# Group 2's second product over 16 row pairs, and five smaller moves, in a fused attention and MLP block

## The chip, the cores and the metric

The kernel runs on one core of a Trainium2 chip. The metric is device time in microseconds (us): the median of several executions of the whole program, from its first to its last instruction. The engines of a core work side by side, each through its own list of instructions in a fixed order, and wait for each other by semaphores: TensorE (PE in the profile; PEld is its loading of the stationary operand), VectorE (DVE), ScalarE (ACT), GpSimd (POOL), and SyncE (SP), which issues most of the DMAs here. A DMA queue is also worked off in order of issue. SBUF is the memory on the chip, with 128 partitions; PSUM is the small memory that matmuls write.

## The reference

One transformer block over 2048 tokens of width 576. LayerNorm, attention over a dilated window of 8 earlier positions (every second one), 32 heads of 18; the projection `wo`; a residual sum; LayerNorm again; an MLP of 4608 columns with GELU (its tanh form); another residual sum.

```python
    def _A_ref(x, wqkv, wo):
        B, S, D = x.shape
        H = 32; Dh = D // H
        W, dil = 8, 2
        qkv = (lambda x, *d: x.transpose(*d))((x @ wqkv).reshape(B, S, 3, H, Dh), 2, 0, 3, 1, 4)
        q, k, v = qkv[0], qkv[1], qkv[2]
        scale = Dh ** -0.5
...
        logits = jnp.einsum("bhsd,bhswd->bhsw", q, kg) * scale
        logits = jnp.where(mask[None, None, :, :], logits, -1e9)
        attn = _softmax(logits, axis=-1)
        o = jnp.einsum("bhsw,bhswd->bhsd", attn, vg)
        return (lambda x, *d: x.transpose(*d))(o, 0, 2, 1, 3).reshape(B, S, D) @ wo

    def _B_ref(x, w1, b1, w2, b2):
        y = _layernorm(x, axis=-1)
        h = _gelu(jnp.einsum("bsd,df->bsf", y, w1) + b1)
        return jnp.einsum("bsf,fd->bsd", h, w2) + b2

    x = A_x
    h = x + _A_ref(_layernorm(x, axis=-1), A_wqkv, A_wo)
    h2 = h + _B_ref(_layernorm(h, axis=-1), B_w1, B_b1, B_w2, B_b2)
    return h2
```

## The kernel before

The 2048 tokens are 16 tiles of 128. A tile j holds every sixteenth token, so that a position two tokens earlier lies in tile j-2, and the window of a tile is made of tiles of the same parity. `kv_ring` holds K and V of the eight even and of the eight odd tiles; after a tile's turn its K or V row is read again from `kv_dram`, shifted by one token (`halo`). The tiles are worked in `ATT_ORDER` (even ones from 14 down, then odd ones from 15 down), two at a time: `GROUPS[0]` is (14, 12), then (10, 8), (6, 4), (2, 0), (15, 13), (11, 9), (7, 5), (3, 1). The first two tiles are called A[0] and A[1] below, the next A[2] and A[3].

The whole order is written by hand, engine by engine, as Python lists of calls that are interleaved with the matmuls.

First come 24 visits (`qd` 0 to 23, L994 to 1000) of two QKV products each. A product of 64 rows of contraction uses half of TensorE, and two such halves run side by side; `visit` (L242) sends the first half of each product (`phase` 0), then the second halves (`phase` 1), which use the other rows. A `marker`, an empty instruction in GpSimd's list, stands between the halves: it waits for the end of a first half, and the second half waits for it. A dictionary gives what is put in: `hooks` between the two halves, `between` behind a second half, `after` behind the visit. ScalarE copies each product from PSUM (L322). In the last visits the attention output o of A[0] and A[1] is turned round by TensorE (`tr_o`, L433), with a copy of its last 64 columns twice side by side (`o_tail`, by ScalarE); Wo follows as a third product of visits 17 and 20; then LN2, the second LayerNorm (`ln2`, `ln2_rstd`, `ln2_norm`: VectorE's statistics, GpSimd's power of -0.5, called the root here, and ScalarE's normalisation), and its output `hn` is turned (`tr_h`, L556) in visits 22 and 23. `transpose_tail` uses 12 matmuls for this: 8 for 512 columns, and 4 for the last 64 columns, which are written once to each half of the partitions.

Then the loop over the groups (L1038), with k = 0 to 7. A group's stage is W1 with GELU (`mlp1`, four visits), Wo of the next group, and W2. In the lists, c and d are the next group's tiles, e and f those of the group after. VectorE meanwhile computes the attention of e and f: `att_qk_a` (products of q and K), `att_qk_b` (sums over the head's width), `att_max` (the maximum and its subtraction), ScalarE's exponential (`exps`), `att_den` (the sum and its reciprocal), then, one group later, `pv_sum` (the products with V), which gives o. `send_o` writes o to DRAM in two stores and `read_o` reads it back turned round (`dma_tr_o` does both), into `oT`, for Wo. LN2 goes the same way: `ln2_h` (h = the projection plus x, by VectorE), `ln2_act` (its sums by ScalarE, its root by GpSimd), `ln2_send` and `ln2_in`. A dependency written by hand keeps the next `att_qk_a` behind the root of LN2 (L354).

W2 is done in two ways. Groups 0 and 1 use 36 row blocks with two matmuls each per tile (`mlp2`, L598). From group 2 on, `mlp2_fast` (L711) takes the blocks in pairs and uses seven products instead of eight, in the manner of Strassen and Winograd, for the first `rows` pairs; the other pairs, up to 18, are done plainly, with 8 matmuls a pair (`plain`). The seven products need sums of blocks of W2 (`w2_sums`, made once) and of h (`h_sums`, made in each group), by VectorE. `t_slot` and `s_slot` say where these are kept. `ROWS` gives 12 pairs for group 2, 16 for groups 3 to 5 and 18 for the last two. `steps` is the order: a tuple is a product and its range of pairs; "wo" is the Wo visit; "b", "d" and "f" are ScalarE's copies of a PSUM bank to the bank in which another product goes on (L782); "hc", "h", "6", "7", "in", "exp", "4" and "3" are places where the lists in `x` are called; "rest" and "o0" are ScalarE's copies of results, "o1" VectorE's sums `o_sb` (L724). Group 2 does product 1 first and Wo behind it; groups 3 to 6 do Wo first.

```python
        ROWS = {2: 12, 3: 16, 4: 16, 5: 16, 6: NM, 7: NM}
...
            if 3 <= k < 7:
                mlp2_fast(g, rows, (s, p, q, r), wo, x, True)
                p, q, r, s = q, r, p, s
            else:
                mlp2_fast(g, rows, (q, p, r, s), wo, x)
```

W2 is loaded in seven parts (`load_w2`). The last one, the row blocks 32 to 35, is issued in group 0, in the list `m1[1]`, between the first and the second half of PV of the group's second tile d.

## Time and profile before

| | |
|---|---|
| median of 3 executions | 360.77 us (360.17 to 361.07) |
| profiled execution, its own time | 361.01 us |
| its span | 359.2 us |
| PE busy, matmuls | 353.4 us (98%), 4953 |
| DVE busy | 295.8 us (82%) |
| ACT busy | 235.8 us (66%) |
| POOL busy | 47.3 us (13%) |
| DMA traffic | 46.29 MB, mean 129 GB/s |

The profile is of one execution. A busy TensorE isn't TensorE at its best, since matmuls overlap: the end of a matmul is modelled, and a short wait shows only as a longer distance between two starts. In a timeline, a row stands for several instructions of one kind, with the start of the first and the time to the end of the last; the number behind x is their count, and a bracket gives the idle time of the engine before it and what ended it. `L228` is the matmul in `phase`, `L605` and `L693` are those of W2, `pq`, `pm`, `pw` and `po` the PSUM tiles of QKV, W1, Wo and W2.

By the windows of the trace, W1 of groups 2, 3 and 4 takes 17.79, 17.80 and 17.78 us (142.38 to 160.17, 178.88 to 196.68 and 214.72 to 232.50), so a group takes some 36 us.

### The profile page before, as it was taken

The numbers are of one execution on the slowest core, as the hardware profiler recorded it, in microseconds if no ns is written. First come the engines' busy times: TensorE is split into PE (matmuls) and PEld (weight loads), VectorE is DVE, ScalarE is ACT, GpSimd is POOL, SyncE is SP. The second block draws the span as 40 slices with busy tenths as digits, with TensorE's granted clock in tenths as the row PEclk, the third lists the DMA queues.
The fourth block names the chain that finished last, engine by engine and source line by source line (L and its number), as shares of the span: only waits on it lengthen the run. The fifth ranks groups of instructions, "written<-read, shape, count | busy, mean of one in ns | idle before, by whom it ended". The sixth has DMA issues, their size and how long they took to land.

```text
span 359.2 us, 11579 instructions
## 1 busy us (share of the span) xinstructions
PE 353.4 (98%) x4953; PEld 289.5 (81%) x4953; DVE 295.8 (82%) x416; ACT 235.8 (66%) x524; POOL 47.3 (13%) x61
## 2 busy tenths in 40 slices
PE   8999999999999999999999999999999999999996
PEld 4777978887788877887788778877887788778874
DVE  5999999999989989998799899989998998520431
ACT  4889757897647783668566956685669566706620
POOL 2241003000212020201200211021102110210000
PEclk9999999999999999999999999999999999999999
DMA  7997799955737584722553545344555253253001
GB/s 242 328 296 168 186 248 294 387 188 137 153 71 123 164 222 84 126 71 49 118 85 82 100 110 84 77 114 108 85 90 102 57 86 56 55 120 51 4 1 34
DMA packets 63492, 46.29 MB, mean 129 GB/s; under 512 B 32192, under 2 KB 61760, under 8 KB 63440
## 3 DMA queue, kind: packets, MB, share of 16 engines
q1 hardware_dynamic: 59472, 41.50, 43.6%
q0 software_dynamic: 3744, 3.84, 9.9%
q8 instruction: 38, 0.62, 0.8%
q10 hardware_dynamic: 224, 0.22, 0.3%
q14 instruction: 14, 0.11, 0.1%
HBM read 23.38 MB, written 12.42 MB: 100 GB/s over the span
## 4 chain that ended last, share of the span: by engine, by line
PE 72%; DVE 20%; DMA 4%; SPq 1%; ACT 1%; issue 1%; DVEq 0%; ACTq 0%
PE pm L228 34%; PE po L693 25%; PE po L605 9%; PE pw L228 4%; DVE prod L361 3%; DVE ln_stats L148 3%; DVE prod L409 3%; DVE prod L352 3%; DVE prod L415 2%; DMA oT<-td 2%; DMA x_all<-in_A_x_dram 1%; ACT h_all L586 1%; SPq L104 1%; DMA td<-q_all 1%; DVE ln_mv L149 1%
## 5 line engine op out<-in xcount | busy, mean ns | idle before, releaser
L228 PE MATMUL pm<-hnT,w_sb 64*128 64x256 bf16 x2304 | 143.0, 269 | 0.0
L586 ACT ACTIVATE h_all<-pm,b_sb 128x256 f16<-128x256 f32 (+1 forms) x288 | 108.4, 495 | 51.2 <-PE pm L228 50.5
L228 PEld LDWEIGHTS <-w_sb 64*128 64x128 bf16 x2304 | 111.7, 94 | 15.1 <-issue 1.7
L693 PEld LDWEIGHTS <-h_all 128*128 128x128 f16 x480 | 46.2, 98 | 13.7 <-issue 1.6
L228 PE MATMUL pq<-wq_sb,xnT 64*128 64x288 bf16 x720 | 54.9, 283 | 0.7 <-DMA wq_sb<-in_A_wqkv_dram 0.2
L228 PEld LDWEIGHTS <-xnT 64*128 64x128 bf16 x864 | 43.4, 94 | 10.9 <-issue 1.4
L361 DVE TENSOR_TENSOR prod<-prod 128x2304 bf16<-128x2304 bf16 (+1 forms) x64 | 44.2, 691 | 2.1
L352 DVE TENSOR_TENSOR prod<-kv_ring,q_all 128x4608 bf16<-128x4608 bf16 x16 | 40.8, 2550 | 2.8 <-POOL ln_rstd L500 2.5
L409 DVE TENSOR_TENSOR prod<-kv_ring,probs 128x4608 bf16<-128x4608 bf16 x16 | 40.9, 2558 | 1.1 <-DMA kv_ring<-kv_dram 0.6
L228 PE MATMUL pm<-hnT,w1h_sb 64*128 64x256 bf16 x288 | 39.2, 269 | 0.0
L693 PE MATMUL po<-w2a_sb,h_all 128*128 128x288 bf16 (+1 forms) x262 | 35.8, 286 | 0.0
L415 DVE TENSOR_TENSOR prod<-prod 128x2304 bf16<-128x2304 bf16 (+1 forms) x32 | 33.9, 1058 | 1.1
L605 PEld LDWEIGHTS <-h_all 128*128 128x128 bf16 x288 | 27.8, 98 | 7.9 <-issue 1.0
L693 PEld LDWEIGHTS <-kv_ring 128*128 128x128 f16 x252 | 24.6, 98 | 6.3 <-DVE kv_ring L673 0.2
L605 PE MATMUL po<-w2a_sb,h_all 128*128 128x288 bf16 x224 | 28.5, 286 | 0.0
L228 PE MATMUL pq<-wqh_sb,xnT 64*128 64x288 bf16 x144 | 27.6, 283 | 0.0
L795 POOL DMA_DIRECT2D x_all<-o_sb x12 | 10.7, 888 | 126.1 <-PE pw L228 73.1
L500 POOL TENSOR_TENSOR ln_rstd<-ln_var,mhalf 128x1 f32<-128x1 f32 x13 | 10.3, 792 | 80.8 <-ACT ln_var L499 80.8
L228 PE MATMUL pw<-wo_sb,oT 64*128 64x288 bf16 x256 | 19.6, 283 | 0.7 <-DMA oT<-td 0.7
L693 PE MATMUL po<-w2b_sb,h_all 128*128 128x288 bf16 (+1 forms) x122 | 19.7, 286 | 0.1
L673 DVE TENSOR_TENSOR kv_ring<-h_all 128x1536 f16<-128x1536 f16 (+3 forms) x9 | 6.8, 760 | 15.8 <-ACT h_all L586 15.8
L161 POOL TENSOR_TENSOR ln_rstd<-ln_veps,mhalf 128x1 f32<-128x1 f32 (+2 forms) x14 | 13.2, 951 | 47.6 <-DVE ln_nmean L489 30.1
(115 smaller groups left out, 401.3 us busy)
## 6 DMA issues: line engine op xcount, KB each, us to landing
w_sb<-in_B_w_dram SPq DMA_DIRECT2D x6, 768.0 KB, 6.1
kv_ring<-kv_dram SPq DMA_DIRECT2D x28, 144.0 KB, 2.3
kv_dram<-kv_ring SPq DMA_DIRECT2D x13, 288.0 KB, 3.7
w2a_sb<-in_B_w_dram SPq DMA_DIRECT2D x3, 1008.0 KB, 10.5
x_all<-in_B_b_dram SPq DMA_DIRECT2D x15, 144.0 KB, 4.1
td<-q_all SPq DMA_DIRECT2D x14, 144.0 KB, 2.0
td<-hn SPq DMA_DIRECT2D x14, 144.0 KB, 1.8
x_all<-h POOLq DMA_DIRECT2D x14, 144.0 KB, 4.6
```

The lines of the kernel that those rows point to most:

```text
L148: nc.vector.bn_stats(out=stats[:, i, c, :], in_=src[:, c * HALF:(c + 1) * HALF])
L161: nc.gpsimd.tensor_tensor(out=rstd[:], in0=veps[:], in1=mhalf[:].to_broadcast([P, n]), op=ALU.pow)
L228: last = nc.tensor.matmul(duo["g"][r ^ swap][i], lhsT=lhsT, rhs=rhs, start=(swap == 0 and i == 0 and kt == 0), stop=(swap == 1 and kt == K ...
L352: ins = nc.vector.tensor_tensor(out=prod[:], in0=k_ring[j % 2], in1=q_all[:, j, :].unsqueeze(1) .to_broadcast([P, W, D]), op=ALU.mult).ins
L361: nc.vector.tensor_tensor(out=prod[:, :, o * H:o * H + n], in0=prod[:, :, a * H:a * H + n], in1=prod[:, :, c * H:c * H + n], op=ALU.add)
L409: nc.vector.tensor_tensor(out=prod[:].rearrange("p w (d h) -> p w d h", h=H), in0=v_ring[j % 2].rearrange("p w (d h) -> p w d h", h=H), in ...
L415: nc.vector.tensor_tensor(out=prod[:, 0:n, :], in0=prod[:, 0:n, :], in1=prod[:, n:2 * n, :], op=ALU.add)
L500: ins = nc.gpsimd.tensor_tensor(out=rstd[:], in0=var[:], in1=mhalf[:], op=ALU.pow).ins
L586: pace[0] = nc.scalar.activation(out=hT(grp)[:, f, 0:N], in_=ps[:, r, i * N:(i + 1) * N], func=ACT.Gelu_apprx_tanh, bias=b1_sb[:, f:f + 1] ...
L605: nc.tensor.matmul(banks[half], lhsT=hT(grp)[:, f, i * P:(i + 1) * P], rhs=w2_rows(f)[:, half * HALF:(half + 1) * HALF], start=(f == 0), s ...
L693: nc.tensor.matmul(bank, lhsT=l, rhs=r, start=start, stop=stop, skip_group_check=True)
L795: nc.gpsimd.dma_start(out=x_of(j), in_=o_of.pop(j), accum_op=ALU.add)
```

## The change

Six things are changed.

- Group 2 uses 16 pairs in the seven products, with Wo first, as groups 3 to 5 do; the order of `steps` and the rotation of PSUM banks are now one for groups 2 to 6. For this the W2 sums of pairs 12 to 15 are all made in group 2, the second tile's QK product goes behind LN2's h and the h sums, and the h sums of pairs 12 to 15 have a place: three slots, two of them in rows of `x_all` that are not yet loaded again (`spare`). The load of x into these rows goes behind the last product of group 2.
- The maximum of the first tile e is taken alone, ahead of the second tile's QK product, in groups 2 to 5; that of f behind it.
- The load of W2's last four row blocks, half of `w2b_sb` (`load_w2(6)`), goes behind the stores and the turned read of o of tile d in group 0.
- `tr_o` of A[0] goes from between the halves of visit 16 to behind the first second half.
- `tr_h` of A[0] goes from between the halves of visit 22 to behind the first second half, and the exponential of A[2] behind the other.
- `tr_h` uses 10 matmuls; the last 64 columns come from a copy, twice side by side, that GpSimd makes (`h_tail`), behind second halves of visits 20 and 22. `transpose_tail` is gone.

```diff
-    def transpose_tail(pair, src):
-        for kt in range(KF):
...
+    def h_tail(j):
+        o_tails[j] = qp.tile([P, 2, HP], BF16, tag="tail", name="tail", bufs=2)
+        nc.gpsimd.tensor_copy(out=o_tails[j][:], in_=hn[j][:, KF * P:D].unsqueeze(1).to_broadcast([P, 2, HP]))
...
     def tr_h(j, tag):
         pair = psum_pair(tag, "h_pt")
-        transpose_tail(pair, hn.pop(j)[:])
+        transpose_in(pair, hn.pop(j)[:], o_tails.pop(j)[:].rearrange("p r c -> p (r c)"))
         nc.scalar.copy(**turned(hnT_slot(j), pair))
...
         if not ring1_free[0]:
-            return q_all[:, 15 - 2 * i, (m0 - SR) * P:(m1 - SR) * P].bitcast(F16).rearrange("p (m c) -> p m c", c=P)
+            rows, j = ((q_all, 15), (x_all, 10), (x_all, 8))[i] if spare[0] else (q_all, 15 - 2 * i)
+            return rows[:, j, (m0 - SR) * P:(m1 - SR) * P].bitcast(F16).rearrange("p (m c) -> p m c", c=P)
...
         if rows < NM:
-            steps = [(1, all_), "b", "wo", "hc", "h", "e", (2, all_), "11", (6, all_), "d", "6", "7", (7, all_), "rest"] if not first_wo \
-                else ["wo", "hc", (1, all_), "b", "h", "e", (7, lo), (2, all_), (6, all_), "6", "d", "rest", "7", "11"] if rows == SR \
-                else ["wo", "hc", (1, all_), "b", "h", "e", (7, lo), (2, all_), (6, all_), "6", "7", "d", "11", (7, hi), "rest"]
-            steps += ["in", (5, all_), "f", "exp", (4, all_), "21", "22", "o1", "4", (3, all_), "12", "o0", "3"]
+            steps = ["wo", "hc", (1, all_), "b", "h", "e", (7, lo), (2, all_), (6, all_), "6", "7", "d", "11", (7, hi), "rest", "in",
+                      (5, all_), "f", "exp", (4, all_), "21", "22", "o1", "4", (3, all_), "12", "o0", "3"]
...
+            16: [c_(tr_o, A[0], "D")],
             18: [c_(o_tail, A[1])],
+            20: [c_(h_tail, A[0])],
...
-            22: [c_(att_exp, A[2])],
+            22: {0: [c_(tr_h, A[0], "D")], 1: [c_(h_tail, A[1]), c_(att_exp, A[2])]},
...
-            16: c_(tr_o, A[0], "D"),
...
-            22: c_(tr_h, A[0], "D"),
...
-        ROWS = {2: 12, 3: 16, 4: 16, 5: 16, 6: NM, 7: NM}
+        ROWS = {6: NM, 7: NM}
...
-                m1[1] = [c_(pv_t, c), c_(att_den, d), c_(att_pv_a, d), c_(halo, d, 2), c_(load_w2, 6), c_(att_pv_b, d),
-                         c_(dma_tr_o, d), c_(add_b2, g[0]), c_(add_b2, g[1]), c_(att_qk_a, e), c_(halo, e, 1)]
+                m1[1] = [c_(pv_t, c), c_(att_den, d), c_(att_pv_a, d), c_(halo, d, 2), c_(att_pv_b, d),
+                         c_(dma_tr_o, d), c_(load_w2, 6), c_(add_b2, g[0]), c_(add_b2, g[1]), c_(att_qk_a, e), c_(halo, e, 1)]
...
-            rows = ROWS[k]
+            rows = ROWS.get(k, 16)
+            spare[0] = k == 2
...
-                              c_(att_qk_a, f), c_(halo, f, 1)]
-                early = {2: (), 5: (0,)}.get(k, (0, 2))
-                if k == 3:
-                    m1[3] += [c_(w2_sums, 12, 14, (2, 3)), c_(w2_sums, 14, 16, (2, 3))]
+                              c_(w2_sums, 12, 14, (2, 3)), c_(w2_sums, 14, 16, (2, 3))]
+                early = (0,) if k == 5 else (0, 2)
...
-                x["7"] += [c_(att_qk_one, f, 1) if k > 2 else c_(att_qk_b, f, 1), c_(att_max, (e, f))]
+                x["7"] += [c_(att_max, [e]), c_(att_qk_one, f, 1), c_(att_max, [f])]
...
-                x["in"] += [c_(reload_x, GROUPS[k + 3])]
+                x["3" if k == 2 else "in"] += [c_(reload_x, GROUPS[k + 3])]
...
-            if 3 <= k < 7:
-                mlp2_fast(g, rows, (s, p, q, r), wo, x, True)
+            if k < 7:
+                mlp2_fast(g, rows, (s, p, q, r), wo, x)
                 p, q, r, s = q, r, p, s
```

More of the change, by code (lines that the diff above doesn't have):

```diff
@@ L183, in transpose_in @@
                                  rhs=ident[half_rows(r), half_rows(r)], start=True, stop=True, skip_group_check=True)
-    def transpose_tail(pair, src):
-        for kt in range(KF):
-            for r in range(2):
-                nc.tensor.matmul(pair[:, r, kt * HP:(kt + 1) * HP], lhsT=src[half_rows(r), kt * P:(kt + 1) * P],
-                                 rhs=ident[half_rows(r), half_rows(r)], start=True, stop=True, skip_group_check=True)
-        for c, rows in ((D - P, slice(None)), (KF * P, half_rows(0))):
-            for r in range(2):
-                nc.tensor.matmul(pair[rows, r, KF * HP:KT * HP], lhsT=src[half_rows(r), c:c + P if rows.start is None else D],
-                                 rhs=ident[half_rows(r), half_rows(r)], start=True, stop=True, skip_group_check=True)
     o_tails = {}
@@ L641 @@
     ring1_free = [False]
+    spare = [False]
     RING_T = 3 * SR * P
@@ L709, in halves, with mlp2_fast @@
         return ap.rearrange("p (g c) -> p g c", g=2)
-    def mlp2_fast(g, rows, tags, wo, hooks, first_wo=False):
+    def mlp2_fast(g, rows, tags, wo, hooks):
         last, summed = wo is None, rows < NM
@@ L1093 @@
                     x["h"] += [c_(h_sums, 0, SR, [t for t in range(4) if t not in early])]
[L1094 to L1096 removed]
+                x["h"] += [c_(h_sums, SR, rows)]
+                x["7"] += [c_(att_max, [e]), c_(att_qk_one, f, 1), c_(att_max, [f])]
                 x["exp"] += [c_(exps, e, f)]
```

3 lines of the change are left out of this document (removed).

## The prediction

> **What bounds the kernel now.** I read the chain that ended last, then the windows of single stages, then the timelines of TensorE (PE), of the DMA queue (SP) and of VectorE (DVE) at the places that the change touches.
>
> ```profile
> PE 72%; DVE 20%; DMA 4%; SPq 1%; ACT 1%; issue 1%; DVEq 0%; ACTq 0%
> ```
>
> The chain is VectorE up to the second o read of group 0 and TensorE from there on. A matmul taken away late in the span is worth its whole time; one taken away early only what TensorE doesn't give back while it waits for VectorE.
>
> ```profile
> 160.17:178.88 18.71, 18.71 (x171) 14.34 (x172) 14.48 (x20) 13.51 (x30) 2.93 (x5) 1.00 0.34 76
> 196.68:214.72 18.04, 18.04 (x166) 14.01 (x164) 16.55 (x25) 13.26 (x29) 2.89 (x5) 1.00 0.51 104
> ```
>
> These are Wo and W2 of group 2 and of group 3 (start:end, length, then busy us and count of PE, PEld, DVE, ACT, POOL, the granted clock, DMA). The clock is 1.00 in both. Group 3 already has the form that the change gives group 2.
>
> **The change part by part.** The sum is made against the profiled execution's 361.01 us (span 359.2); it lies 0.24 above the median of 360.77, inside the runs' 360.17 to 361.07, so I take the gain off the median.
>
> *Seven products over 16 pairs, Wo first.* Group 2 needed 7x12+8x6 = 132 W2 matmuls; with 16 pairs it needs 7x16+8x2 = 128, as group 3 does. Wo directly behind W1 also saves one change between half-height and full-height matmuls. The two windows price both together: 18.71-18.04 = **0.67 saved**, between 0.5 (four of some 0.124, the spacing in the next fence) and 0.67.
>
> *W2's last half behind an o read.* The store of o's tail and the read that waits for it, for the first and the second tile of group 0:
>
> ```profile
> 84.86 4.83 PE L605 MATMUL po<-w2a_sb,h_all 128*128 128x288 bf16 x38
> 90.06 0.66 PE L228 MATMUL pw<-wo_sb,oT 64*128 64x288 bf16 x8 [0.37 <-DMA oT<-td]
> ```
> ```profile
> 77.37 0.71 SPq L211 DMA_DIRECT2D td<-q_all  x1
> 79.23 1.21 SPq L216 DMA_TRANSPOSE oT<-td  x1
> ...
> 83.99 0.42 SPq L211 DMA_DIRECT2D td<-q_all  x1
> 87.24 1.21 SPq L216 DMA_TRANSPOSE oT<-td  x1
> ```
>
> From store to read it takes 1.86 for the first tile and 3.25 for the second, which stands behind W2's load. Without the load in front the read starts 1.39 sooner and oT lands near 88.7. TensorE's 38 rows end about 84.86+38x0.124 = 89.6: the wait of some **0.44 goes**, while TensorE comes less than 0.9 sooner itself. The load is then issued near 87.1, past two stores and the read; its rows are used from about 94 (13 rows of 0.25 behind the Wo visit). If it were later than that, TensorE would wait one for one. Behind it in the queue are K's halo, a bias row and two halo stores; the halo is read only by the next tile's QK product, with the QK additions of this tile in between.
>
> *Transposes and tails.* The last two visits of QKV, on TensorE and ScalarE:
>
> ```profile
> 63.61 0.29 PE L228 MATMUL pq<-wqh_sb,xnT 64*128 64x288 bf16 x2
> 63.97 0.67 PE L228 MATMUL pq<-wq_sb,xnT 64*128 64x288 bf16 x8
> ```
> ```profile
> 62.70 0.67 ACT L559 CAST hnT<-h_pt 128x640 bf16<-128x640 f32 x1
> 63.27 0.65 ACT L322 ACTIVATE q_all<-pq 128x576 bf16<-128x576 f32 x1
> ...
> 65.09 0.69 ACT L559 CAST hnT<-h_pt 128x640 bf16<-128x640 f32 x1 [0.33 <-PE h_pt L192]
> ```
>
> TensorE's second matmul at 63.61 should be followed in 0.12; it waits 0.25 for the bank that the copy at 63.27 frees, because the cast of hnT goes first. The change turns the two round and takes 12 transposes to 10 per tile. ScalarE then loses its idle 0.33 before the second cast, and W1 of group 0 can't start before that cast ends: **0.35 saved**, between 0 and 0.5. The exponential of the third tile now stands behind one more copy; VectorE reads it only in group 0.
>
> The o transposes, one visit half later:
>
> ```profile
> 45.24 0.31 PE L228 MATMUL pq<-wqh_sb,xnT 64*128 64x288 bf16 x2
> 45.65 0.29 PE L182 MATMUL o_pt<-ident,q_all 64*128 64x64 bf16 x8
> ```
> ```profile
> 58.66 0.28 PE L228 MATMUL pq<-wqh_sb,xnT 64*128 64x288 bf16 x2
> 58.91 0.67 PE L228 MATMUL pq<-wq_sb,xnT 64*128 64x288 bf16 x8
> ```
> ```profile
> 54.23 2.86 POOL L161 TENSOR_TENSOR ln_rstd<-ln_veps,mhalf 128x1 f32<-128x1 f32 x1 [26.38 <-DVE ln_nmean L489]
> ```
>
> At 45.65 TensorE has waited some 0.3 for o; that wait is filled. But at 58.91 it waits again, for a bank whose copy stands on ScalarE behind LN2's normalisation, and this behind GpSimd's root, which ends at 57.09 by VectorE's order. TensorE comes there sooner and waits longer: I cost the moved o transposes at **nothing**, between 0 and a gain of 0.4.
>
> The tails go to GpSimd, between the markers that let TensorE change halves. No copy by GpSimd is in the trace; the nearest rows are a 128x128 write and the root above, 0.3 to 2.9 us:
>
> ```profile
> 1.08 0.29 POOL masks.py:199 TENSOR_SCALAR_AFFINE_SELECT ident<-ident 128x128 bf16<-128x128 bf16 x1
> ```
> ```profile
> 62.14 0.60 DVE L376 TENSOR_REDUCE peak<-logits 128x32 f32<-128x256 f32 x1
> 62.77 0.43 DVE L377 TENSOR_TENSOR logits<-logits,peak 128x256 f32<-128x256 f32 x1
> 63.11 2.55 DVE L352 TENSOR_TENSOR prod<-kv_ring,q_all 128x4608 bf16<-128x4608 bf16 x1
> ```
>
> LN2's second normalisation ends near 62.8, so the second tail starts about 62.9, ahead of the long QK product. I take 0.3: done before TensorE's second transposes at about 64, cost nothing. If it came behind the product's start, the first rival holds.
>
> *A maximum sooner; VectorE in groups 2 to 5.*
>
> ```profile
> 159.45 2.55 DVE L352 TENSOR_TENSOR prod<-kv_ring,q_all 128x4608 bf16<-128x4608 bf16 x1
> 163.61 1.42 DVE L475 TENSOR_TENSOR h<-pw,x_all 128x576 f32<-128x576 f32 x2 [1.61 <-PE pw L228]
> 164.95 0.95 DVE L673 TENSOR_TENSOR kv_ring<-h_all 128x1536 f16<-128x1536 f16 x1
> ...
> 176.04 0.95 DVE L724 TENSOR_TENSOR o_sb<-po,o_sb 128x288 f32<-128x288 f32 x2 [2.21 <-ACT warm L562]
> ...
> 195.91 0.39 DVE L663 TENSOR_TENSOR kv_ring<-w2a_sb,q_all 128x576 f16<-128x576 bf16 x1
> ...
> 204.92 2.56 DVE L352 TENSOR_TENSOR prod<-kv_ring,q_all 128x4608 bf16<-128x4608 bf16 x1 [1.01 <-POOL ln_rstd L500]
> ...
> 212.75 0.94 DVE L724 TENSOR_TENSOR o_sb<-po,o_sb 128x288 f32<-128x288 f32 x2
> ```
> ```profile
> 232.84 0.29 PE L228 MATMUL pw<-woh_sb,oT 64*128 64x288 bf16 x2
> 233.41 0.66 PE L228 MATMUL pw<-wo_sb,oT 64*128 64x288 bf16 x8 [0.29 <-DMA oT<-td]
> ```
>
> In group 3 VectorE idles 1.01 before the second tile's QK product, for the root. The first tile's maximum (0.60+0.43) fits there, so the logits of group 3 are done about 0.6 sooner. The o_sb sums at 212.75 follow without idle time, so half a microsecond of that reaches group 4's o, and TensorE's wait at 233.41 (0.57 from start to start where 0.12 is usual) goes: **0.45 saved**, between 0 and 0.45. Groups 4 and 5 show no such wait to save. Group 3 also loses the four W2 sums from 195.91 on, some 1.4 us at this row's size.
>
> Group 2 gets these 1.4 us, four more h sums of a third of the 0.95 row's columns (between 0.3 and 0.5 each: about 1.5) and about 0.3 for maxima in two pieces: 3.2 us against idle 1.61 and 2.21. They fit, but unevenly: the four W2 sums and two early h sums (0.95 each) now stand before LN2's h, the QK product of 159.45 behind it. I get VectorE free for h at 159.45+1.4+1.9 = 162.75, less some 0.5 for the earlier o of group 0, thus 162.2; TensorE, 0.8 sooner, has then done Wo (36 matmuls, 2.2 us, from 160.17-0.8) near 161.5. That is 0.7 behind TensorE; in group 3, where no wait stands before h, I take 0.2 or so. What is queued behind h is ScalarE's LN2 and then the bank copy that seeds product 5:
>
> ```profile
> 206.43 0.38 ACT L782 COPY po<-po 128x288 f32<-128x288 f32 x1
> ```
>
> In group 3 that copy ends at 206.8, and TensorE comes to product 5 after Wo and 68 matmuls, about 196.68+2.2+8.4 = 207.3: 0.5 to spare, here 0.5 less, and the markers and bank copies in between can only add. I take **0.3 lost**, between 0 and 0.7 (this holds group 2's hnT too, for which TensorE comes some 0.8 sooner and LN2 0.5). The halo behind the QK product now follows LN2's stores in the queue, and x for group 5 is loaded only after product 3; neither is read before the next group.
>
> Sum: 0.67+0.44+0.35+0.45-0.3 = 1.6 us. 361.01-1.6 = 359.4 for a profiled execution, 360.77-1.6 = **359.2** for the median.
>
> **The rivals.**
> *A tail behind the product.* The root at 54.23 took 2.86 us because it started with a QK product. If the second tail starts behind 63.11 it is done at about 65.66+0.4 = 66.1; TensorE's second transposes, the markers queued behind the copy and the cast (0.69) wait, and W1 starts near 67.0 instead of 65.9 (behind the cast of 65.09). That is 1.1 late; the o wait hides 0.44 of it, 0.67 and 0.45 come back later and the 0.3 isn't lost: about 360.3. For it: only 0.2 us separate the two starts. Against: VectorE's order there doesn't change. The Trainium skill (SBUF — State Buffer, "SBUF: two separate sides") says that VectorE and GpSimd lock a shared port pair for a whole instruction, whichever starts first. By that rule the subtraction at 62.77, with two inputs from SBUF, holds the copy off until the product is due, and this rival decides; the 2.86 of the root agrees with it.
>
> *VectorE of group 2 too late: slower.* The o_sb sums start 2.84 before the stage's end in group 2 (176.04) and 1.97 in group 3, where group 4's o came 0.45 late. So group 3's o has 0.42 to spare. If none of the 3.2 us fell into the idle time and TensorE is 1.1 sooner, VectorE 0.5, o comes 3.2+0.6-0.4 = 3.4 late; 0.3 of it is taken already: 359.2+3.1 = 362.3. It decides once those sums of group 2 start later than 2.4 before the stage's end, and my own sum comes close to that. Against: two idle stretches of 3.8 us, and group 3 with 16.55 busy of 18.04.
>
> *The o read is no sooner.* If the 3.25 comes from something other than the load in front, 0.44 stays: 359.6.
>
> **How the numbers follow.** Forecast 0.58, tail behind the product 0.17, VectorE too late 0.10, o read no sooner 0.15. About 0.3%, 1.1 us, is what a measurement can tell: faster is below 359.7, slower above 361.9. Faster: nearly all of the forecast and over half of the last, 0.65; same 0.26; slower 0.09. The forecast's bounds are 358.3 (no loss in group 2, the o transposes' 0.4, 0.5 for the cast) and 359.8; up to the tail's 360.3 and some way toward the slower case: 358.3 to 360.6.
>
> **What would show it.** Right: W1 of group 0 starts near 65.6; no wait for oT in groups 0 and 4; group 2's stage of Wo and W2 takes about 18.3; GpSimd's copies take 0.3 to 0.6. Wrong: a copy of 2 us or more with TensorE idle at 64; a wait for oT in group 3; a gap over 0.7 before product 5 of group 2; a wait for w2b_sb near 94.

## The result and the profile after

The changed kernel takes 359.34 us (median of 6 executions, 359.12 to 359.69), the kernel before beside it 360.56 (6 executions, 360.17 to 361.07): a ratio of 0.996, with a 95% interval of 0.9949 to 0.9972. The forecast was 359.2. The change makes the kernel faster, by 0.4%: the interval lies below 1. The profiled execution took 359.3 with a span of 357.5, against 361.01 and 359.2.

The page's chain of waits, after:

```profile
PE 51%; DVE 39%; ACT 3%; issue 2%; DMA 2%; SPq 1%; POOL 0%; DVEq 0%; POOLq 0%; ACTq 0%
```

TensorE has 51% of it instead of 72%, VectorE 39% instead of 20%. So somewhere late in the program the chain now leaves TensorE for VectorE. The starts of W1 tell how much time each group takes (us from the start of the span, first W1 matmul of each group):

| W1 of group | 0 | 1 | 2 | 3 | 4 | 5 | 6 | 7 | end |
|---|---|---|---|---|---|---|---|---|---|
| before | 65.98 | 104.57 | 142.31 | 178.82 | 214.66 | 250.90 | 286.69 | 322.34 | 359.23 |
| after | 65.44 | 103.65 | 141.40 | 177.58 | 213.51 | 249.30 | 285.08 | 320.62 | 357.52 |
| gained in the step | 0.54 | 0.38 | -0.01 | 0.33 | -0.09 | 0.45 | 0.01 | 0.11 | -0.01 |

A group's step runs from its W1 to the next W1, so that 0.38 is that of group 0, 0.33 that of group 2, 0.45 that of group 4. They sum to 1.71; the forecast was 1.6. The medians differ by 1.22 only: the profiled execution of the kernel before lies 0.45 above its median. Group 6's 0.11 is a read of o that lands 4.4 after its issue in the trace before and 2.8 after it in the changed kernel; no edit touches that read. The views of these places follow in the order of time.

*The last visits of QKV*, by the timelines of TensorE, ScalarE and GpSimd:

```profile
58.20 0.29 PE L222 MATMUL pq<-wqh_sb,xnT 64*128 64x288 bf16 x2
58.95 0.67 PE L222 MATMUL pq<-wq_sb,xnT 64*128 64x288 bf16 x8 [0.47 <-ACT kv_ring L316]
...
62.37 0.21 PE L182 MATMUL h_pt<-ident,tail 64*128 64x64 bf16 x2
62.40 0.65 PE L222 MATMUL pq<-wq_sb,xnT 64*128 64x288 bf16 x7
...
65.14 0.28 PE L222 MATMUL pq<-wqh_sb,xnT 64*128 64x288 bf16 x1
65.44 0.61 PE L222 MATMUL pm<-hnT,w_sb 64*128 64x256 bf16 x8
```
```profile
64.69 0.70 ACT L553 CAST hnT<-h_pt 128x640 bf16<-128x640 f32 x1
```
```profile
58.43 0.56 POOL L193 COPY tail<-hn 128x128 bf16<-128x128 bf16 x1 [1.29 <-ACT hn L174]
...
62.90 0.51 POOL L193 COPY tail<-hn 128x128 bf16<-128x128 bf16 x1 [1.29 <-ACT hn L174]
```

ScalarE's second cast has no idle time before it, GpSimd's copies take 0.51 and 0.56, and W1 starts at 65.44, 0.30 behind the last QKV matmul's start, by the second cast. The wait at 58.95 has grown, as forecast.

*The o read of group 0*, by the timelines of the DMA queue and of TensorE:

```profile
84.16 0.42 SPq L205 DMA_DIRECT2D td<-q_all  x1
85.81 1.21 SPq L210 DMA_TRANSPOSE oT<-td  x1
87.11 0.53 SPq L104 DMA_DIRECT2D w2b_sb<-in_B_w_dram  x1
```
```profile
84.34 4.83 PE L599 MATMUL po<-w2a_sb,h_all 128*128 128x288 bf16 x38
89.10 0.67 PE L222 MATMUL pw<-wo_sb,oT 64*128 64x288 bf16 x8
```

From store to read it takes 1.65 instead of 3.25, and Wo starts without an idle time that the trace shows. W2's load is issued behind it, and TensorE doesn't wait for it.

*Group 2*, by the timelines of VectorE, ScalarE and TensorE:

```profile
160.24 0.95 DVE L669 TENSOR_TENSOR kv_ring<-h_all 128x1536 f16<-128x1536 f16 x1
161.23 0.96 DVE L669 TENSOR_TENSOR h_all<-h_all 128x1536 f16<-128x1536 f16 x1
162.10 1.41 DVE L469 TENSOR_TENSOR h<-pw,x_all 128x576 f32<-128x576 f32 x2
...
175.29 0.95 DVE L720 TENSOR_TENSOR o_sb<-po,o_sb 128x288 f32<-128x288 f32 x2 [0.30 <-PE po L689]
```
```profile
162.88 0.68 ACT L491 ACTIVATE hn<-h 128x576 bf16<-128x576 f32 x1 [0.85 <-DVE h L469]
...
164.79 0.39 ACT L776 COPY po<-po 128x288 f32<-128x288 f32 x1
...
169.35 0.38 ACT L776 COPY po<-po 128x288 f32<-128x288 f32 x1
```
```profile
163.36 1.63 PE L689 MATMUL po<-w2a_sb,h_all 128*128 128x288 f16 x12
165.24 1.88 PE L689 MATMUL po<-w2a_sb,h_all 128*128 128x288 bf16 x14 [0.24 <-ACT po L776]
```

Here is the new wait, and where the chain leaves TensorE. The 12 matmuls at 163.36 are product 7; product 2 should follow them 12 x 0.123 = 1.48 later, at 164.84, and comes at 165.24. It goes on in a PSUM bank that ScalarE must first have copied (step "b"). That copy, at 164.79, stands on ScalarE behind the LN2 work that begins at 162.88, and this stands behind VectorE's h at 162.10, which waits for nothing but the two h sums in front of it. The third row of ScalarE is the copy "d", which seeds product 5, of which I had said that it comes late: it was in time.

*Groups 3 and 4*, by the timeline of TensorE, where Wo changes from the first to the second tile's o:

```profile
195.76 0.29 PE L222 MATMUL pw<-woh_sb,oT 64*128 64x288 bf16 x2
196.03 0.66 PE L222 MATMUL pw<-wo_sb,oT 64*128 64x288 bf16 x8
```
```profile
231.70 0.29 PE L222 MATMUL pw<-woh_sb,oT 64*128 64x288 bf16 x2
231.82 0.65 PE L222 MATMUL pw<-wo_sb,oT 64*128 64x288 bf16 x8
```

In group 4 the distance is the usual 0.12, where it was 0.57. In group 3, which had no such wait, it is 0.27. Group 4's gain isn't what it seems; the experiments come back to it.

### The profile page after: what moved, and what is told of

Same layout as the page of the kernel before. It is cut to its first block, busy times and chain, and to the rows that moved or that the text cites. A ratio compares the mean times of both kernels' runs of the same rounds, so it can differ in the third digit from the quotient of the medians.

```text
span 357.5 us, 11586 instructions
## 1 busy us (share of the span) xinstructions
PE 351.9 (98%) x4945; PEld 291.5 (82%) x4945; DVE 298.5 (84%) x428; ACT 235.8 (66%) x524; POOL 48.4 (14%) x63
## 4 chain that ended last, share of the span: by engine, by line
PE 51%; DVE 39%; ACT 3%; issue 2%; DMA 2%; SPq 1%; POOL 0%; DVEq 0%; POOLq 0%; ACTq 0%
PE pm L222 24%; PE po L689 24%; DVE prod L355 7%; DVE prod L346 6%; DVE prod L403 6%; DVE prod L409 5%; DVE ln_stats L148 3%; PE pw L222 3%; DMA x_all<-in_A_x_dram 1%; DVE den L397 1%; DVE h L469 1%; ACT h_all L580 1%; SPq L104 1%; DVE peak L370 1%; DVE q_all L410 1%
## 5 line engine op out<-in xcount | busy, mean ns | idle before, releaser
L222 PEld LDWEIGHTS <-w_sb 64*128 64x128 bf16 x2304 | 113.2, 94 | 13.8 <-issue 1.6
L689 PEld LDWEIGHTS <-h_all 128*128 128x128 f16 x464 | 44.7, 98 | 13.4 <-issue 1.8
L689 PE MATMUL po<-w2a_sb,h_all 128*128 128x288 bf16 (+1 forms) x252 | 34.2, 286 | 0.2 <-ACT po L776 0.2
L689 PE MATMUL po<-w2b_sb,h_all 128*128 128x288 bf16 (+1 forms) x112 | 18.8, 286 | 0.2 <-DVE h_all L669 0.2
```

The lines of the kernel that those rows point to most:

```text
L222: last = nc.tensor.matmul(duo["g"][r ^ swap][i], lhsT=lhsT, rhs=rhs, start=(swap == 0 and i == 0 and kt == 0), stop=(swap == 1 and kt == K ...
L689: nc.tensor.matmul(bank, lhsT=l, rhs=r, start=start, stop=stop, skip_group_check=True)
```

## The experiments

Executions differ in when VectorE's first sum for a reciprocal (`den`) starts: at 37.97 to 38.85 in the profiled ones. Of what differs between these kernels only one warm-up lies before that, so the traces are compared from there. All times in this table are us after that start; the last column is the step from W1 of group 2 to W1 of group 3.

| kernel | W1 of 0 | W1 of 1 | W1 of 2 | W1 of 3 | end | step of group 2 |
|---|---|---|---|---|---|---|
| before | 27.17 | 65.77 | 103.51 | 140.02 | 320.42 | 36.50 |
| changed kernel | 26.60 | 64.81 | 102.55 | 138.73 | 318.67 | 36.18 |
| the same, another execution | 26.60 | 64.79 | 102.54 | 138.72 | 318.52 | 36.18 |
| load back | 26.60 | 65.65 | 103.39 | 139.20 | 318.98 | 35.81 |
| transposes and tails back | 27.17 | 65.34 | 103.08 | 138.88 | 318.97 | 35.80 |
| maxima together | 26.60 | 64.80 | 102.55 | 138.79 | 318.58 | 36.25 |
| group 2's part alone | 27.18 | 65.60 | 103.34 | 139.17 | 318.96 | 35.83 |
| tails by transposes | 26.93 | 65.09 | 102.84 | 138.68 | 318.61 | 35.84 |
| o transposes back | 26.59 | 64.81 | 102.55 | 138.70 | 318.67 | 36.15 |
| second tail copied twice | 28.21 | 66.37 | 104.11 | 139.90 | 319.81 | 35.79 |
| longer warm-up | 26.61 | 66.29 | 104.03 | 139.84 | 319.79 | 35.81 |
| one h sum later | 26.59 | 64.80 | 102.54 | 138.33 | 318.12 | 35.78 |
| the same, another execution | 26.78 | 64.98 | 102.72 | 138.51 | 318.29 | 35.78 |
| one h sum later, maxima together | 26.59 | 64.80 | 102.54 | 138.32 | 318.10 | 35.78 |

Two executions of one kernel differ by 0.15 to 0.17 at the end by this count.

### The load of W2 back in front of the o read

```diff
-c_(att_pv_b, d), c_(dma_tr_o, d), c_(load_w2, 6),
+c_(load_w2, 6), c_(att_pv_b, d), c_(dma_tr_o, d),
```

> The changed kernel with the load of W2's last four row blocks back between the halves of PV, ahead of o's stores. Theory: up to 90 us the second o of group 0 sets TensorE's time, so both the load's move and the transposes' 0.54 are lost: oT lands near 90.1, TensorE waits about 0.9 ahead of the second Wo product (none with the change), W1 of group 1 starts near 104.5 instead of 103.65. Rival (the parts add up, the move is worth its own 0.4 only): W1 of group 1 near 104.1. Of what is lost, group 2 gives some back if its own wait of 0.40 comes from VectorE: TensorE comes later there, the wait falls under 0.1; time 359.8 to 359.9 for a profile, against 360.2 if that wait stays.

The median is 359.55 (12 executions), the ratio to the kernel before 0.9981, interval 0.9969 to 0.9994. TensorE's timeline in this kernel:

```profile
89.45 0.66 PE L222 MATMUL pw<-wo_sb,oT 64*128 64x288 bf16 x8 [0.81 <-DMA oT<-td]
```

The read is late again, and TensorE's idle time is 0.81, more than the 0.37 of the kernel before, since TensorE arrives earlier by what the transposes gave while o comes when VectorE and the queue let it. W1 of group 1 is 0.84 later than with the load moved (65.65 against 64.81). At the end of the program 0.31 to 0.46 of this is left, because the wait of group 2 is not there: its step is 35.81. I had expected the same 0.85 at W1 of group 1 and some 0.5 to 0.6 at the end.

That the load's place makes the read late is shown: from store to read it takes 3.00 to 3.25 in the three traces with the load in front, 1.64 to 1.79 in ten of the eleven others. How it does so is not. In this trace 120 of the 128 small packets of the store run by 85.02, and with the load moved behind (the second trace of the changed kernel, whose store is issued at the same 83.62) all of them by 84.81; the last 8 here run from 85.83 on. A packet of 16 KB on the DMA queue that the profile calls `instruction`, a packet of instructions below, runs from 84.14 to 85.07; with the load moved behind it ran from 82.80 to 83.72. In all three traces with the load in front such a packet begins 0.5 to 0.7 behind the store's issue. The eleventh of the others, the second tail copied twice, has one too, 0.11 behind the issue, and takes 2.78 without any load in front. So the load may hold the store up by moving this packet onto it, and not by standing ahead of it in the queue.

### The transposes and the tails back, alone

```diff
-16: [c_(tr_o, A[0], "D")], ... 22: {0: [c_(tr_h, A[0], "D")], 1: [c_(h_tail, A[1]), c_(att_exp, A[2])]},
+22: [c_(att_exp, A[2])], ... 16: c_(tr_o, A[0], "D"), ... 22: c_(tr_h, A[0], "D"),
-transpose_in(pair, hn.pop(j)[:], o_tails.pop(j)[:].rearrange("p r c -> p (r c)"))
+transpose_tail(pair, hn.pop(j)[:])
```

> The changed kernel with both transposes, their tails and the exponential as before (no copies by GpSimd). Theory: W1 of group 0 starts at 65.98 instead of 65.44, no wait for oT in group 0 (the read lands at 88.7, TensorE comes at 89.6), W1 of group 1 near 104.15; in group 2 TensorE comes 0.5 later against VectorE and its wait of 0.40 is gone, so the whole loses only about 0.1: 359.4. Rival (0.54 is worth 0.54 at the end): 359.8, with the wait in group 2 still there.

The median is 359.04 (5 executions), the ratio 0.9964, interval 0.9953 to 0.9976. W1 of group 0 starts 0.57 later, at 27.17, as in the kernel before; W1 of group 1 is 0.53 later, W1 of group 3 only 0.15 later. Between the two lies group 2, whose step is again 35.80. The end is 0.30 to 0.45 later, where I had expected 0.1: group 6 takes 35.83 in this trace and 35.54 in the changed kernel, since a read of o lands 4.8 after its issue.

### Group 2's part alone

This is the changed kernel with the load, the transposes, the tails and the maxima as before; only the 16 pairs, the order of products and the W2 sums of group 2 are new (the edits above, and the one below).

> Group 2's 16 pairs alone: the changed kernel with the load, the transposes, tails and exponential, and the joint maximum as before. Theory: Wo and W2 of group 2 lose 0.67 against before with no wait or one under 0.1 (TensorE and VectorE come there as before), group 3 gains no wait over 0.3; if the W2 sums' leaving group 3 suffices, group 4's 0.45 goes too: 361.01-0.67-0.45+0.2 = 360.1 for a profile; if it needs the early maximum: 360.5. Rival (the extra sums of VectorE make group 2 late by themselves): a wait of 0.4 or more in group 2, 360.8 or later.

The median is 359.26 (6 executions), the ratio 0.9967, interval 0.9955 to 0.9979. The end is 1.46 sooner than in the kernel before, out of the change's 1.75 to 1.90. This is more than the 0.9 that I had expected: 0.17 of it comes in group 0 and 0.12 in group 6, where this kernel is the one before, so that much differs between executions. Group 2's step has hardly a wait (35.83). Group 4's, which is 35.78 in this trace and 36.25 in the kernel before, has none: the wait for o in group 4 went without the early maximum.

### The maxima together again

```diff
-x["7"] += [c_(att_max, [e]), c_(att_qk_one, f, 1), c_(att_max, [f])]
+x["7"] += [c_(att_qk_one, f, 1), c_(att_max, (e, f))]
```

> The changed kernel with one maximum for both tiles behind the second QK product, as before. Theory of the prediction: the maximum ahead fills VectorE's idle 1.0 us and removes group 4's wait for oT; without it that wait of about 0.45 is back, and group 3's grows from 0.15 to about 0.55: 359.3+0.85 = 360.1. Rival: the W2 sums that left group 3 already make VectorE wait for TensorE there (o_sb sums idle 0.9 before them with the change, none before), so group 4 has no wait without the early maximum either; group 3's 0.4 alone: 359.7.

The median is 358.74 (5 executions), the ratio 0.9952, interval 0.994 to 0.9964: not slower. VectorE's timeline has the idle time ahead of group 3's QK product again, and groups 3 and 4 have no wait all the same (group 4's step, from 213.09 to 248.87, is 35.78, and so is group 3's):

```profile
202.80 2.56 DVE L346 TENSOR_TENSOR prod<-kv_ring,q_all 128x4608 bf16<-128x4608 bf16 x1 [1.09 <-POOL ln_rstd L494]
```

So the maximum sooner is worth nothing that these traces show. Two other things set the kernel before apart at group 4's wait. First, the tail of o is stored 12.33 after W1 of group 4 there, and 11.94 to 11.96 after it in the thirteen other traces. The four W2 sums, which the change takes from group 3's VectorE (0.39 to 0.45 each) into group 2's, would explain that, but they were not put back by themselves. Second, the store is slow. The queue's timeline and the DMA view of 226.9 to 230.6 in the kernel before, and the queue of the changed kernel:

```profile
226.99 0.42 SPq L211 DMA_DIRECT2D td<-q_all  x1
230.56 1.20 SPq L447 DMA_TRANSPOSE oT<-td  x1
```
```profile
q8 instruction: 1, 0.02, 2.4%
```
```profile
225.45 0.43 SPq L205 DMA_DIRECT2D td<-q_all  x1
227.05 1.47 SPq L441 DMA_TRANSPOSE oT<-td  x1
```

From store to read it takes 3.57 in the kernel before, 1.60 in the changed kernel and 1.60 or 1.61 in eleven more traces. The packet of instructions in the view begins at 228.02 and takes 1.40. The one trace left is that of the longer warm-up, below, which tells the two things apart.

### One h sum of group 2 behind LN2's h

```diff
-early = (0,) if k == 5 else (0, 2)
+early = {2: (2,), 5: (0,)}.get(k, (0, 2))
```

> The changed kernel, but in group 2 one of the two h sums that stand ahead of LN2's h (0.95 us) goes behind it. Theory: TensorE's wait of 0.40 us ahead of product 2 of group 2 comes from VectorE, which reaches LN2's h at 162.10, some 0.5 after Wo is done; with one sum less in front VectorE reaches h about 0.5 sooner, ScalarE's first bank copy ends about 164.7, and the wait goes: the period from W1 of group 2 to W1 of group 3 falls from 36.18 to 35.8 or 35.9. VectorE then idles some 0.4 ahead of h and ends its group 0.4 later; if that brings waits for oT in groups 3 and 4, part of the gain is given back there (up to 0.4). Median between 358.9 and 359.3. Rival (the copy is late because of ScalarE's own work, not of h): the period stays at 36.1 to 36.2 and the median at 359.3 or above.

The median is 358.20 (6 executions, 357.97 to 359.61), the ratio 0.9957, interval 0.9943 to 0.997. The timelines of VectorE, ScalarE and TensorE in this kernel:

```profile
160.50 1.41 DVE L469 TENSOR_TENSOR h<-pw,x_all 128x576 f32<-128x576 f32 x2
```
```profile
163.19 0.39 ACT L776 COPY po<-po 128x288 f32<-128x288 f32 x1
```
```profile
162.58 3.35 PE L689 MATMUL po<-w2a_sb,h_all 128*128 128x288 f16 x26
```

Product 7 and product 2 are now one row of 26 matmuls without a stop, and the copy is done half a microsecond before it is needed. The step of group 2 is 35.78, 0.40 less, so the wait came from what stood ahead of h on VectorE. The idle time of 0.4 that I expected on VectorE is not there: the row of h, at 160.50, names none. Nor has this trace a wait in group 3. The median lies 0.7 below the range that I had expected; it was taken on another chip than the changed kernel's, beside a kernel before of 360.28.

### The same with the maxima together

The two edits above in one kernel.

> The same with the maximum of both tiles taken together behind the second QK product, as before the change. Theory (the early maximum is worth nothing, and the wait of group 2 can be had back): group 2's period 35.8 to 35.9, no wait for oT over 0.15 us in groups 3 and 4, the end 0.3 to 0.4 sooner after the first reciprocal than with the joint maximum alone (318.6 to about 318.2), median about 358.3 to 358.5, the fastest of all. Rival (VectorE has no room left, and each delay of it comes back as a wait for oT): group 3 or 4 waits 0.3 or more and the median stays at 358.7 or above.

The median is 358.30 (5 executions), the ratio 0.995, interval 0.9939 to 0.9962. The steps of groups 2, 3 and 4 are 35.78 each, and the end is 0.48 sooner than with the maxima together alone (318.10 against 318.58). VectorE's room was enough. It is not the fastest by the median, as I had expected, but its end is the soonest of the table, by 0.02.

### Both again on one chip

The changed kernel and the one with the later h sum, side by side.

> The changed kernel again, on the same chip as the version with one h sum of group 2 behind LN2's h, so that the two can be compared without the change of chip. Theory (the wait ahead of product 2 is worth about half a microsecond to the end): this one 0.3 to 0.7 us above the other by the medians, its period of group 2 36.1 to 36.3 against 35.8. Rival (the start of an execution varies more than that, and the difference seen before was one of chips): the medians lie within 0.2 us.

> The changed kernel with one of group 2's two early h sums behind LN2's h, again, beside the changed kernel on the same chip. Theory: 0.3 to 0.7 us below it by the medians, about 1.7 to 2.3 below the kernel before, with no wait for an o read or a bank copy over 0.15 us in groups 2 to 5 of the trace. Rival: within 0.2 us of the changed kernel.

Here the medians say nothing for the later sum: 358.96 (8 executions, ratio 0.9946, interval 0.9928 to 0.9964) and 358.90 (6 executions, ratio 0.994, interval 0.9919 to 0.9961). The rival is right on that. The traces repeat what they showed: a step of group 2 of 36.18 with the wait, of 35.78 without; nor is a wait left in groups 3 to 5 of the latter's trace, as expected. But the end of the changed kernel was 0.15 sooner this time, since group 3 didn't wait (35.78), and the other's W1 of group 0 started 0.19 later (26.78 against 26.59). Gaps of some tenths early in an execution, which this edit doesn't touch, are as large as the 0.40: VectorE's first sum for a reciprocal starts at 38.85 and 38.33 in the two traces of the changed kernel, at 38.07 and 38.71 in the two of the other. That the later sum is the faster version is shown for its stage, not for the whole time.

### The second tail copied twice

The same copy is made once more ahead of the one that counts, so that this one starts later.

```diff
+if j == ATT_ORDER[1]:
+    nc.gpsimd.tensor_copy(out=o_tails[j][:], in_=hn[j][:, KF * P:D].unsqueeze(1).to_broadcast([P, 2, HP]))
```

> The changed kernel with the second tile's tail copied twice by GpSimd, so that the copy that counts stands 0.5 us later and starts at about 63.4, behind the start of the long QK product (63.2 to 65.8). The prediction's first rival: that copy is held to the product's end, lasts 2 us or more by the trace, and W1 of group 0 starts 1 us or more later than with one copy (28.0 us or more after the start of the first reciprocal's sum, where it is 26.6). If the copy runs beside the product, it is done near 64.0, and W1 of group 0 starts where it did (26.6 to 26.8).

The timelines of GpSimd, VectorE and TensorE in this kernel:

```profile
62.94 2.51 POOL L195 COPY tail<-hn 128x128 bf16<-128x128 bf16 x1
```
```profile
62.65 2.64 DVE L348 TENSOR_TENSOR prod<-kv_ring,q_all 128x4608 bf16<-128x4608 bf16 x1
```
```profile
65.50 0.20 PE L182 MATMUL h_pt<-ident,tail 64*128 64x64 bf16 x2 [1.61 <-POOL tail L195]
```

The copy that starts 0.29 behind the product's start ends at 65.45, 0.16 behind the product's end, and TensorE stands idle for 1.61. W1 of group 0 comes 1.61 later, the end 1.14 to 1.29. That is the first rival of the prediction, at about its price: it had the end 1.1 late (360.3 against 359.2) and W1 1.1 late, by 0.5 too little; the 0.40 that group 2 gives back here made up for most of that. One execution took 359.90.

### The o transposes back between the halves

```diff
-16: [c_(tr_o, A[0], "D")],
+16: c_(tr_o, A[0], "D"),
```

> The changed kernel with the first tile's o transposes back between the halves of their visit. The prediction costed this move at nothing, because the wait that it takes away comes back at the last visits, where the bank copy stands behind LN2's normalisation. Theory: W1 of group 0 starts where it did (26.6 us after the sum of the first reciprocal, within 0.1), and the wait ahead of the visit at 58.9 shrinks from 0.64 to some 0.2. Rival (the move is part of the 0.54 that the start gained, which the prediction put at 0.35): W1 of group 0 starts 0.15 to 0.3 later.

TensorE's timeline at the later visit:

```profile
58.62 0.29 PE L222 MATMUL pq<-wqh_sb,xnT 64*128 64x288 bf16 x2
58.88 0.67 PE L222 MATMUL pq<-wq_sb,xnT 64*128 64x288 bf16 x8
```

The distance here is 0.26 instead of the changed kernel's 0.75, and W1 of group 0 starts at the same time (26.59). One execution took 359.26. The move is worth nothing by itself.

### The tails by transposes, the moves kept

> The changed kernel with the last 64 columns of LN2's output turned by four matmuls per tile again (12 transposes per tile), and no copies by GpSimd; the transposes stay where the change put them. The start of W1 in group 0 gained 0.54 us from transposes and tails, where the prediction had 0.35 from the order of the casts and nothing from the copies. Theory: the two transposes less count little (some 0.1 for both tiles), so W1 of group 0 starts 26.6 to 26.8 us after the sum of the first reciprocal (26.6 with the copies, 27.18 with the old places). Rival (the tails are most of the gain): 26.9 or later.

`transpose_tail` is back and `h_tail` gone. TensorE's timeline:

```profile
62.13 0.36 PE L192 MATMUL h_pt<-ident,hn 64*128 64x64 bf16 x4
62.42 0.66 PE L232 MATMUL pq<-wq_sb,xnT 64*128 64x288 bf16 x7
```

The four transposes of a tail hold TensorE for 0.29, from their start to the next visit's (0.27 for the second tile); the two of the change for 0.03 (62.37 to 62.40). For two tiles this is 0.50, of which the changed kernel waits 0.18 for the cast again (0.30 at 65.44 instead of 0.12). W1 of group 0 is 0.33 later, so the tails are more than half of the 0.57: the rival is right. The other 0.24 is the order of the casts. At the end nothing of it is left (318.61 against 318.52 and 318.67); one execution took 358.99.

### A longer warm-up, to move TensorE's program

The kernel begins with 40 small matmuls instead of 8 long and 8 small ones. They only warm TensorE. One execution took 359.79.

```diff
-for n in [512] * 8 + [P] * 8:
+for n in [P] * 40:
```

> The changed kernel with 40 small matmuls at its start that only warm TensorE, in place of 8 long and 8 small ones: 24 matmuls with their weight loads more, so that every later instruction of TensorE stands 48 places further on in its program. In the changed kernel a packet of 16 KB on a queue of instructions begins at 189.92 and takes 1.70 us, while the tail of o is stored in group 3 (189.46); the read that waits for the store starts 3.64 us after it, where 1.9 to 2.6 is usual. Theory: that packet is TensorE's next piece of program and holds up the store's small packets; 48 places further on it is fetched 1.4 to 3 us sooner, clear of the store, which then takes 2.0 to 2.7 from store to read, TensorE's wait for oT at 195.8 (0.14) goes, and group 3's period falls from 35.94 to 35.8; other stores may be hit instead. Rival (the store is slow because of the K read and the 144 KB store beside it, or because VectorE's o is late): the packet moves, the store still takes 3.3 to 3.7, and the period stays at 35.9. The wait of group 2 (period 36.2) stays by both.

The reason to look was group 3's o in the changed kernel. The queue's timeline, and the DMA view of 189 to 192:

```profile
189.46 0.42 SPq L205 DMA_DIRECT2D td<-q_all  x1
193.10 1.21 SPq L441 DMA_TRANSPOSE oT<-td  x1
```
```profile
q8 instruction: 1, 0.02, 3.5%
...
td<-q_all SPq DMA_DIRECT2D x1, 16.0 KB, 3.6
```

With the longer warm-up the same two views (190.5 to 193) have no row for a queue of instructions, and the store is quick, landing 1.6 after its issue:

```profile
191.00 0.42 SPq L205 DMA_DIRECT2D td<-q_all  x1
192.64 1.21 SPq L441 DMA_TRANSPOSE oT<-td  x1
```

From store to read it is 1.64 instead of 3.64, and the wait for o in group 3 is gone. But "1.9 to 2.6 is usual" was wrong: in group 3 the thirteen other traces take 2.71 to 3.72, each with such a packet beside the store. And the packet hardly moved (189.46 instead of 189.92); it was the store that came 1.5 later, so this is no clean test of the place in the program. And two of my numbers were wrong: the step of group 3 is 35.86, not 35.8, since 0.08 is lost ahead of product 2 there (0.20 from start to start instead of 0.12), and group 2's wait went too. The cause of the latter is a new wait in group 0, by TensorE's timeline and the DMA view of 78.5 to 83.2:

```profile
83.16 0.66 PE L222 MATMUL pw<-wo_sb,oT 64*128 64x288 bf16 x8 [1.33 <-DMA oT<-td]
```
```profile
q8 instruction: 1, 0.02, 1.5%
...
oT<-td SPq DMA_TRANSPOSE x1, 4.6
```

A packet of instructions falls into the first o read, which takes 4.6 to land. In the changed kernel the same read took 2.9 with no such packet in its time:

```profile
oT<-td SPq DMA_TRANSPOSE x1, 2.9
```

TensorE then comes to group 2 1.5 later (104.03 against 102.55) and finds the bank copied.

Other stores may be hit instead, I had written, and group 4's is:

```profile
225.89 0.42 SPq L205 DMA_DIRECT2D td<-q_all  x1
229.50 1.21 SPq L441 DMA_TRANSPOSE oT<-td  x1
```

The packet begins at 226.27 here, and from store to read it takes 3.61, as in the kernel before. But o is stored 11.96 after W1 of group 4, not 12.33, and the distance where Wo changes from the first to the second tile's o is 0.18, where it was 0.57; the step is 35.86. So a slow store with an early o costs 0.08, and the 0.47 of the kernel before takes both, the slow store and the late o. With the usual 1.60 the read would start 1.97 sooner, and there would be nothing to wait for, late o or not.

## Why the prediction was right, and where it was not

**Group 2: 0.67 saved and 0.3 lost, 0.33 measured.** Both terms have their size: where the wait is absent the step is 35.78 to 35.84, 0.66 to 0.72 less than before, and the wait is 0.40. Its cause is the one that was given, VectorE late at LN2's h (162.10; I had worked out 162.2) with ScalarE queued behind. The step that failed is the last link, "the bank copy that seeds product 5": it is the copy before it, on which product 2 waits, 4.6 us sooner. I had followed ScalarE's list past the nearer copy, although "b" stands right behind LN2's first work.

**W2's load: 0.44 forecast, 0.38 measured**, with the read, the landing and the load where they were expected. The rival that something other than the load makes the read late is ruled out as far as the load's place goes; that the load did it by standing ahead in the queue is not shown. The sum held only in its order: the load was counted on top of the transposes' 0.35, and the two do add up at W1 of group 1, but undoing the load alone costs 0.84 there, since the transposes' gain would run into the same wait.

**Transposes and tails: 0.35 forecast, 0.54 measured.** The term was mis-sized, because I priced ScalarE's idle time and not TensorE's: the two transposes less per tile are 0.26 and 0.24, by their rows. The order of the casts, which was to bring the whole 0.35, brought 0.24 of the 0.57, and the tails, priced at nothing, 0.33. The moved o transposes are worth nothing, for the reason given.

**Group 4: 0.45 forecast, 0.45 measured, for the wrong reason.** The wait went, but the early maximum did not do it: the trace without it has no wait either. The step that failed is the reading of the wait before: the prediction took o as late through VectorE alone and did not look at the store, which took 3.57 there instead of 1.60. "Group 3 also loses the four W2 sums" fits the 0.37 to 0.39 by which o is stored sooner since, and with a slow store that is worth most of the 0.45 (0.08 is left in the longer warm-up); with a quick store it is worth nothing. The kernel before was traced once, so whether its other executions wait there is open, and that the number came out is luck.

**Group 3: not forecast, 0.09 lost** in the profiled execution. The prediction had named a wait for oT in group 3 as a sign of being wrong, and 0.14 of it came. Two things make it: o is stored 11.88 after W1 of group 3 instead of 11.39, which VectorE's added work in group 2 would explain, and the store takes 3.64 instead of 3.05. In the second trace of the same kernel o is stored 11.88 after W1 as well, the store takes 3.43, and the wait is gone.

**What the sum left out.** The load and the transposes bring 0.79 at W1 of group 1 (65.60 against 64.81), and 0.29 to 0.44 at the end. Group 2's wait takes 0.35 of it (36.18 against 35.83): it is only there when TensorE comes early enough, with both. Undo either and it is gone. The forecast's loss of 0.3 stood for this. That the whole came out near is partly luck: the transposes' excess and group 6's 0.11 hide group 3's loss, group 4's 0.45 hangs on one slow store, and the gain is 1.71 by the two profiled executions and 1.22 by the medians beside each other (1.93 in the later runs of both kernels, 360.89 against 358.96).

**The rivals.** The tail behind the product is a real mechanism, missed by little. VectorE's timeline of the changed kernel beside the copy of 62.90:

```profile
62.83 0.42 DVE L371 TENSOR_TENSOR logits<-logits,peak 128x256 f32<-128x256 f32 x1
63.17 2.64 DVE L346 TENSOR_TENSOR prod<-kv_ring,q_all 128x4608 bf16<-128x4608 bf16 x1
```

The copy starts 0.27 before the product's record. By the Trainium skill (SBUF — State Buffer, "SBUF: two separate sides") the subtraction from 62.83 on should hold the copy off; the trace agrees in that it ends at 63.41, 0.16 behind the subtraction's end, just as the late copy of the experiment ends 0.16 behind the product's. What was wrong is my step from there, that the product then goes first: the copy took its turn and the product's record is 0.09 longer (2.64 against 2.55). VectorE too late was to decide "once those sums start later than 2.4 before the stage's end". They start at 175.29, 2.29 before it, and with the maxima together 1.94 before it (175.37 against 177.31), with no wait in groups 3 and 4 of that trace: the point was set too early.

## What to carry to other kernels

A gain upstream is worth what the next late engine leaves of it: before adding up terms, ask at each later stage how much earlier TensorE may come before another engine's work sets its time, and take the smaller. When a step on the path is late, follow the lists of all engines behind it to the *first* user, not to the tightest one that comes to mind. When several edits share a stage, undo them one at a time: a wait that only their sum makes shows in no single one. And before a wait in one trace is put down to an engine, look at the same transfer in other traces: here a store that took twice its usual time stood behind it.

## What the runs showed of the hardware

Packets of 16 KB on the queue `instruction`, 0.88 to 1.98 us each, run beside the kernel's own transfers, 38 in a trace and 39 with the longer warm-up. Where one fell beside the small packets of an o store or a turned read, these took some 1 to 2 us longer. In group 4 the store took 3.57 and 3.61 from issue to read in the two traces in which a packet began 1.03 and 0.38 behind the issue, and 1.60 to 1.61 in the twelve others; in group 3 it took 2.71 to 3.72 in the thirteen traces with a packet beside it and 1.64 in the one without; a read landed after 4.6 instead of 2.9. It is not the only cause of a slow store: in group 2 the second tile's store takes 3.3 to 4.3 in all fourteen traces, thirteen of them with no such packet beside it. At 189.92 such a packet took 1.70; of the store's 128 packets of 128 bytes 120 ran from 190.40 to 190.63, and the last 8, a sixteenth, which is one of the 16 engines' share, from 192.36 on. That the packet held them up is read from this order, not shown by taking it away.

GpSimd's copy of 128 x 128 takes 0.50 to 0.56 us when it gets its turn between two of VectorE's instructions, and 2.51 when it starts just behind a product's start.
